# Attention with a SwiGLU gate: the first phase's maxima beside the last two projection blocks

## The chip, the cores and the metric

The kernel runs on one core of one Trainium2 chip. The metric is the device time of one execution in microseconds; of several executions the median counts. Besides them there is one profiled execution, whose time and trace are used for all reasoning about single instructions. The engines are called as in the profile: PE is the matrix engine, PEld its weight loads, DVE the vector engine, ACT the scalar engine, POOL the GpSimd engine, SP the engine that issues nearly all DMAs.

## The reference

The input is one sequence of 2048 rows of 512 numbers, normalised per row; all data are float32.

```python
def _A_ref(x, wqkv, wo):
    H = 32; Dh = D // H                       # 32 heads of 16
    qkv = (x @ wqkv).reshape(B, S, 3, H, Dh).transpose(2, 0, 3, 1, 4)
    q, k, v = qkv[0], qkv[1], qkv[2]
    scores = jnp.einsum("bhqd,bhkd->bhqk", q, k) * Dh ** -0.5
    p = _softmax(scores, axis=-1)
    o = jnp.einsum("bhqk,bhkd->bhqd", p, v)
    return o.transpose(0, 2, 1, 3).reshape(B, S, D) @ wo

def _B_ref(x, w1, w3, w2):                    # 512 -> 1792 -> 512
    return (_silu(x @ w1) * (x @ w3)) @ w2

xn = _layernorm(x)
return x + _A_ref(xn, wqkv, wo) * _silu(_B_ref(xn, w1, w3, w2))
```

Products are made of split operands: a number is kept as a high part that PE takes as it is and a low part, and a product is three matmuls (low by high, high by low, high by high; `split3`, line 184).

## The kernel before

**Opening.** Lines 345 to 481 work through four blocks of 512 rows. A block has eight projections to queries and keys (12 matmuls of 128x128 by 512 each, lines 444 to 455) and four to values (`token_values`, 12 matmuls, line 410), in the order: two projections, then one value product, four times. Behind a query or key projection ACT copies the high part out of PSUM (line 452), DVE subtracts it for the low part (line 453), and both go to DRAM over SP's queue (line 455). Blocks 0 to 2 also turn the next block's normalised rows (`transposed`, line 389). The transposed rows of a block lie in a pair of tiles, for even blocks in the opening's own pool, for odd blocks in the pool `keep`; they also go to DRAM (line 440) for the gate. `load_k` and `load_q` (lines 327 and 335) bring a head pair's keys and queries back from DRAM in six DMAs each: after block 2 the queries of pairs 0 and 1 (lines 480 and 481), in block 3 keys and queries of pair 0 and keys of pair 1 (lines 474 to 478).

**Attention.** A phase is a pair of heads and half of the queries, 32 phases in all. Head 0 of a pair works on the upper 64 rows of the array and head 1 on the lower 64 rows, so two matmuls of 64 rows run at once, in two lanes. A phase needs first its row maxima: 64 matmuls (`max_unit`, line 488), each reduced by DVE out of its PSUM bank into the tile mp (line 498). `max_rows` (line 501) joins them, turns them with PE (line 510), splits them into high and low (lines 513 and 514) and writes them with four SP DMAs as two more rows under the queries of each head (line 521). Only then the phase's 64 score matmuls can run (`scores`, line 523, they use these rows), each followed by an exponential on ACT into one of 13 tiles pt (line 533). Four exponentials make one chunk for the product with the values (`values`, line 538, accumulated in the bank pv). At the end of a phase `take_out` (line 546) copies pv to the tile ot and divides it by the sums, over several DMAs, POOL splits it (lines 567 and 568).

**Gate.** Beside attention, `gate` (line 608) is cut into half matmuls of 64 rows for the same two lanes (`Lanes`, line 702; matmul at line 757). Its weights come in 168 units of 128x512: an SP DMA (line 282), then two POOL operations that make high and low (`Weights.pump`, lines 296 and 297) in a ring of nine tiles each (`w_split`, line 206, tile pool `ring`). At most AHEAD = 5 units are split ahead.

**Closing.** The last phase (pair 15, second half) is run so that its two query halves are finished one behind the other; between them the output projection (`projecting`, line 934, 12 matmuls for each of 16 row tiles), the product with the gate and the writing of the result take place. Its inputs are fetched by `tend` in a fixed order once the last gate matmul is out (`open_tail`, line 797).

**PSUM.** Seven banks are handed out by `take` (line 156): the one that is free earliest by the kernel's own estimate, the one longest unused among equals. In the opening that is a plain rotation. The eighth bank is pv.

**Order.** What PE gets after the opening, and so the order on all engines, is written out by hand in `ORDER_OF_ISSUE` (line 44), one letter for each item: f and F a half matmul of the gate in lane 0 and lane 1, m and M one of the maxima, s and S one of the scores, v one chunk by values, R a phase's rows turned and written, r is R and v, o one tile of the output projection. A dot emits nothing: it advances the clock of `Model` (line 211), an estimate kept while the kernel is built, with which an item that is not possible yet is held back until it is (line 1124). All engines execute their instructions in the order in which they were emitted; PE waits at a matmul whose data or bank aren't ready. Memory of the opening's pool is taken over by the pools `ring`, `work` and `ffn`, whose first use waits for the last use of the old tiles, DMAs out of them included.

Of the kernel before, what the change touches and what calls it, by code (L numbers as in the profile page):

```python
# [49 lines left out]
    "MvSmMffSfFfSFffMsFsFMfsFfFmFsFFfmSfFmFmFvsMSssMvMmsSfMvsMSffMSffMfSSffMfMrSfMssFfFmFFfFmFsFsFfmFmFFm"  # L50
    "SfFfFmFsFfmSvsMMfmSvvMsfMfSFffSfFmSfFfMfSFfsFMfsFfMMfvsMMsfSvSsMsmFmFvSmFfFsFmFsFfmSfFFmmFSffFmFsFFf"
    "fMsFFffMsFfFmFmFFfSfMmvSfMfMfSfMfMfSfvSmfMMsfSvsMsMmMvvSffMSfMfSfFfSffMsFfFsFmFsFmFFfsFmFvsMSsvmSfSf"
    "FmSFffFmSfFsFFsmFfFSmfFSfFfMsFfSfMRvMsSmFmFmvSmFmMsvsFFsMmFmsFvSmMfFsmFFfFsFfMfSsFfFfMfFsFmSfFfMfsFF"
    "mFmFfMfMsvSmSmmFvmFsFFmFmSsvvsMfSSfmFfFFfSmfFMfSfSfFfMfsFsSvMsMmFmvvSfMfSfSfMffSfMfMfFfFsFsFmFmFfFsF"
    "sFmFFmFfSsvMsSmfMfMvSsMmvsMfSMfFffSFfmSfFfSmFFfSfmFFsFsMfFfmFsMfFMsvsMmMFsvvMfsFfSFmSffFMfFsFfsFMfmF"
    "SfFffSmFsFfSmFRvsMSfMsvFmmSMfvSfMfMsFsfFfFSfmFsFFfmSFfFmsFmFfFSmfFfMfMvvMffSMffSsFFfmFSfFmFfFsFmSfSf"
    "FmFfsFmFsFvSmSfsSMfvMfSsMfMfvSmMsfMvsMSffSmFfFfFmSfFmFsFmFfFsFmFfFFfMmmMvvsMsFFsFsFsFmSvMfSffMfFSfMf"
    "fSfMfFFsMfFsmFFfSfmFMvSmMmSsvSmFmFssFmFFffSFfSmFfSfFmsFFfMmFfsFMfMfvvsMsSSfrMsSfMfMmvsMMsfFFfFfsFfMF"
    "sFfFsMfSffFSmFffSmFFmFfMmvSmfSMmvsMMsFsvsMFmSfFfFsFfMfSfFmFfSfMfmFSfFfSfMfmFsFFmMvvSmSmSmvSffMMsfFsF"
    "FffSmFsFfFmFSfmFsFSffFMffFmFMsvsMMfSmvsMSsFmmFvMsFsFmFsFfFmsFfFmFSfMfSfMffFMmFfMmvvSffMfMMfSsvSmSfMf"  # L60
    "FfSffFMsFfSfMffSfFsMFffFsMfSfFFmFfsFmFSfmFrsMsMMsvsMsSvMsSmfMfMvvsMfSfMfSfMffSfSfMfSFfmFFfsFmFsFsFFf"
    "mMvvmSFfFsfMSffFmFfFSfmFsFFsMfFfSfMfFfsFmFSfsFvvSmMssMvsMSfMfFfSffFmFSffFmSSfFfmFsFFfmSfFSfFmFfFmsMv"
    "sMMfMsvsMsFsFMffFfFMsFfFsMffFSfMmvSmmFmFFsvvSmfSMfFfFsfFfMmFSffFSfsFfMFffMsFFmFfsMvSmFmFsmFvSmmSSfFf"
    "fFfFMsfFsFsFFfSfMfSfrvSmSsMsvmMsSmFvSmmFsFfSFfFfMsFfSfmFSffFmFsFmFmFvvmFSmfSSfFffFmFFsfFmFsFsFSsvvsF"
    "FsMsFfMfFfSffFSmFfFsMffSFfsMFfsFMffFmFMmvvSmsFmFFmmFSsFfFFfFsMfSffMfSFfsFmFmFmSvSmMmmSvvsMMffSfSfSfS"
    "MvMsMfsFFfsFFfsMFfFsFmSfFfMsFfSfMfFfSfMmFfFmMvvsMMfMsvsMfMSfSfFfFmfFSfmFSfSfmFFfSfMfFsFmmFFsFmFsFRvm"
    "SSmmMvSsmMvSmMfsFFffSFfMffSfFMsFsFffMsFfFSfMfmFmFFmvsMmFFsFmvMsmSmFsFvvsMSsMffFfFfMsFfFFmfSfSmFSfFfm"
    "MvvSfMffSSfSffMfMsFFfFfFsmFFssFmFFfFssFMfFfsMvMfSfSfSmvMsSmSmvsMSfmFSfFffMSfFfmFsFFsmFmFFfsFmFfFMfMf"
    "sMvSfmSmMvsMfSMmvvSmsFFsmFfFfMSfsFFfMfMfsFfSfFMfSfMfsFMfFsFmRvSmmFSmvvSmFsFfsFFmFfSfFmfFFsmSFfFfsMFf"
    "SfMffMfFmSvsMsSMmvmSfSfMfMvSmmFsFfFFfFsFfSfMfSfFfMsFfFsfMsFfFmMvsMMmFmvvmSSfSfMfFfFfmSFfFsmFsFFfsFmF"  # L70
    "fFsSFfMffSsFvMmsMMfvsMSsvMsfMsFSffFfSmFfFsMFfSffFmSfFFmFsfFFmSsFfmMvMsfMMsvvSfmSfFFfMffFSfFmmFfSFffS"
    "FfMfSffMsFFsfFmFSfFfMsRvsMSmmSvSmMsMfsvsMMmvvSfMfMffSMffSfSfMfFfFsmFFsMfFffSFmSffFMfsFfFMsFmfFsMfFmF"
    "sFfFMsvmMfSSmfFFffFSfmFmFsFvvsMsMMsvsMSffSfMfFfFfMSfMffSfSfFMfsFFfsFmFmFsFFmvSmSfMmvSmmMvSmmFsFfFfFS"
    "fFmsFmFsFfFMfsFfMFfMmvsMmMsFvsMFfmSFfSffFsMfFsFmFfSfFsMfFfFMfsFMfSmvSsMsvMmSmvSmfFfFsFFmfSmFFfSfmFsF"
    "fMfFSfMfmFfSRvMssSsMvMfSmfSfFmFFfsFmFFfmSvSmmFSmvvmFsFFmfFFsFmmFsFFfFsFmFsFfFmfSSfMffMvSmsSSmvmSFsfF"
    "mFfFsFMfFsfFmSFfsFMfSfFfMsFfMfFfvmSsMMmvvsMMffSfSfMffSfSmFfFFsFmFffSmSFfmFfFSfmFsFmFFmvsMsMsFvsMsMMs"
    "vvsMSffSMffFfFSfMfFmSfSffFmFSffFmFsFmFFmmFsFrvSmSffFMfFsFfsMfFsFmFFsFfmSFfSfSfmFfFmMvsMSfMsfMvSmSsmM"
    "vsMmMFsvvMfSmfSfFSfFfMffSfFMsfFsFMfsFFsMfFmFFssFvvMsMfSffSfMfSfmFfFSfmFsFfFmFsFfFmSmFFfSfFmfFmSvSmSm"
    "mMvvsMsFsFMfFfFfsFMsFfsFMffFSsFfMfFfMfSfMfSmFFmMvvSsMsmSvFmSmmFsFFffFSfFmFfSfFmfSFfFmSfMfmFMfFfsMvsM"
    "MfMsvvSmSfSfMffFFfMsfFSfmFsFfFMsfFmFFsfFsFSfRvSmsSMfvsMmMsFvvMsfFfMfSfFSfmSfFFfsMfFSffFmSFfsFmFsFFfm"  # L80
    "SvMsFmsFsFvvMsFfSffSMffFfSFsmFFfmSfFfSFfmFfSmFFmvMsSsMmvsMfMmMvSsMfFffFfSfMfSfMsFFfMfsFfFmMsFfFmMfFS"
    "mFFmFvSsFmMmvSmmFSmvSmFmFsfFFsFmFsFfMfSfMfFsMffFSffMfFSfMfMmvvSmMfsFFfsFFfMsFfsFMfFfSfSmFfSfFmFfSfSf"
    "mFfFMsRvsMsMMsvvMsMsfMfMvSfSfMffSMffMmvSmSfsFFfFmFfsFFmsFFfSmfFmFSffSfFMsFffFmSFfSfMfsFfFMmvMsMfMfSf"
    "vSfsMsSvmSfMfFfFsFmFMsvsMmMsFvvsFfFFsfMFssFmFfFSfMfSffFmSfFmFmFSffFSmvsMmSmFvsMfFsSMfFffFsMfFsFSfMff"
    "FsMfFSffFmMvvsSmSfFfFmFFffSfMfSfFmSfFmFfFsMfFmSvSmfMsMvsMfMfSfFfSfFmFmFsFmFsFfFsFsFmFsFrvsMfSfSfMfSv"
    "mSsMMmvsFFsFmmFFsFmFsFfSffFmFmFSfSfMffFMfSfFmFsFfSfmFvmFsMmFfSvsSsMmFvsSmFmFFsvvSmfSfMSffFFfMsFfsFmF"
    "sFFfMsFfMfFsfSfFmMFfmMvvSmfSmFFsfFFmFsFmFsFmFfSfSfFmFffSfSMfSfsFMfvmSfSMmvSmmMFsFmvsFMffFSffMFssFmFf"
    "FSffSMffFMfSfmFfFsFvMsMmFsvsMsMFmrSmMsvSmMfFsfFfSFfmSfFFmSffSfFfMFsFfmFfSfFMmvsMsSmFFmvvMsFsfFfMFsFf"
    "mFSffFMsfFSfMfFfsFMsFfMfMfvsMmSmSvsFmSmFmFvSmFffSFfFmSffFmSfFSfmFsFfFMsfFfSMffSvMssMMsvSmmMfFFsfFFfs"
    "FFmFsmFFfsFmFfFMfMfMsvSsMfMmvsMMfMfMffSvSfMsFffFFsMfMfSfSffFFsmFFfmFsFFfMfSmvSmSsvMsSmrsMMfmFFmvsMfS"  # L90
    "mFFffSFfmFsFFfFmSmFffSfMfFSfmFfSmFfFmMvvSmsSmFFfFfFmFsFsFmfFsFFmFsFmMvsMMsSffMvMfSfMffSSffMfMvSffMsS"
    "sFvMssFFsfMFffFMsfFfSfMfSFfsMFfSmFmFFfSmvSmMmmFvvSmSfmFfFFfFsmSfFSfmFFfFsFmFsFfMsFfSfMfSfvMsMsMmvvSf"
    "MfMfSffMfSsFfFMfsFsFFfMmFfMsvsMFfSfmFmFSmFfmFmFvvRSmmSFfFfFfsFFmsFFsFmFsfFFsMfFsMvmSfMfSfMfSfSMffSfM"
    "fMfSfsvsMsSMmvvsMSffSfSfSfMmvfMsFmFfFsFFmFsmFFmFsFfFsmFFfsFFmSfFmfFSfmFFsmFFfMsvSsMsmMvvSfMfSfMffMfM"
    "MfSfMffSvvSffSfMfMfSfSfMfsFFfsMFfsFMfsFFfmSFfmFFmfSfFsMvsMmMvSmFffSmFfSfFfMSfFmFmsFFfmFsFfFfMFmvSmMm"
    "sFsFvsFmMMsvsSmSfFfFmFFsfFmFFsfFSmfFFmFfSmfFMfSRvsMsMMfvSmSsvmSMsFffFfSfFMfSfMffFSffFMsfFSfMsvMfSmFm"
# [12 lines left out]
    "fmFMmvvSfmFFfSfFsSfmFfFFsFmFfFsmFmFFfmSvSmMfSfSsvMsMfmSfMvvSffMfSSffMfMsMffMsfSffFsFmFsFmFsFFfmFsFmF"
# [25 lines left out]
def raw(ap):  # L135
    return ap.bitcast(F32)
# [1075 lines left out]
```

## Time and profile before

| what | us |
|---|---|
| median of three executions | 1814.79 (1814.16 to 1815.48) |
| the profiled execution, its own time | 1813.45 |
| the span of its trace, first to last instruction | 1811.2 |
| opening ends, first matmul of the maxima | 156.07 |
| first score matmul | 205.56 |
| last matmul of the maxima | 1702.3 |

The trace counts from the first instruction, so the profiled execution's own time is 2.25 us over the span, and it lies 1.34 us under the median of the three. In the rows below a time in front is the start in the span, the next number the duration, "x" the number of instructions, and square brackets hold the idle time of the engine before the instruction and what ended it. A row of a table by stretches has the stretch, its length, and for each engine its busy time with the number of instructions, then the granted PE clock (PEclk, 1.00 is full), the share of the DMA engines and GB/s. With a line chosen, the engine columns of that table count that line alone. Matmuls overlap, so what counts on PE is the distance from start to start.

### The profile page before, as it was taken

To read this page: it belongs to the slowest core of one execution; us is meant where nothing else is said; L and a number is where in the kernel's file an instruction comes from. 1 tells how busy PE (TensorE), PEld (TensorE's weight loads), DVE (VectorE), ACT (ScalarE), POOL (GpSimd) and SP (SyncE) were. 2 spreads that over 40 slices of the span, in tenths; PEclk is the share of its full clock that TensorE was granted. 3 is DMA by queue.
4 is the path that set the end of the run, shared out by engine and by line. 5 is a ranking of instruction groups with operands and counts; after the bars stand their busy time and mean duration, and the time that the engine had idled before them with its cause. 6 is when DMAs were issued, how large, how long until landed. Compare 5 with 4: busy or idle time off the path is not lost.

```text
span 1811.2 us, 35399 instructions
## 1 busy us (share of the span) xinstructions
PE 1777.9 (98%) x13136; PEld 1034.9 (57%) x13136; DVE 1472.7 (81%) x2450; ACT 1247.7 (69%) x2360; POOL 696.7 (38%) x728
## 2 busy tenths in 40 slices
PE   7999999999999999999999999999999999999998
PEld 6886755555555555555555555555555555555445
DVE  6525988889888898888899888899888888999525
ACT  3221477777777777776787777777777778777742
POOL 2104932545055523544255505551345425542000
PEclk9999999999999999999999999999999999999999
DMA  6656212122231213132222203222313121222542
GB/s 229 239 168 168 68 39 46 53 58 68 71 91 53 60 42 72 49 66 92 55 76 56 56 25 74 52 65 90 89 45 69 48 64 42 66 74 68 176 143 87
DMA packets 130203, 147.27 MB, mean 81 GB/s; under 512 B 28016, under 2 KB 86384, under 8 KB 126960
## 3 DMA queue, kind: packets, MB, share of 16 engines
q1 hardware_dynamic: 129744, 144.51, 28.7%
q8 instruction: 103, 1.69, 0.4%
q14 instruction: 68, 0.56, 0.1%
q10 hardware_dynamic: 288, 0.52, 0.1%
HBM read 104.33 MB, written 39.58 MB: 79 GB/s over the span
## 4 chain that ended last, share of the span: by engine, by line
PE 89%; DVE 6%; issue 2%; POOL 1%; DMA 1%; ACT 1%; SPq 0%; DVEq 0%; POOLq 0%; ACTq 0%
PE pv L543 25%; PE f L757 24%; PE e L530 17%; PE m L496 13%; DVE mp L498 5%; PE e L186 2%; PE e L190 2%; PE e L188 2%; PE m L186 1%; PE m L188 1%; PE m L190 1%; PE o L186 1%; PE o L188 1%; PE o L190 1%; DVE ot L564 1%
## 5 line engine op out<-in xcount | busy, mean ns | idle before, releaser
L498 DVE TENSOR_REDUCE mp<-m 128x1 f32<-128x512 f32 x2048 | 1296.3, 684 | 172.5 <-PE m L496 89.3
L533 ACT ACTIVATE pt<-e 128x512 f32<-128x512 f32 x2048 | 1091.6, 608 | 351.4 <-PE m L496 158.2
L530 PE MATMUL e<-qs,ks 64*128 64x512 f32 x2048 | 733.5, 419 | 2.8 <-DVE mp L498 2.4
L496 PE MATMUL m<-ks,qs 62*128 62x512 f32 x2048 | 723.0, 418 | 3.7 <-DVE mp L498 2.1
L543 PE MATMUL pv<-pt,vt 128*17 128x512 f32 x4096 | 524.0, 599 | 4.4 <-ACT ot L1088 3.9
L530 PEld LDWEIGHTS e<-qs,ks 64*128 64x128 f32 x2048 | 342.2, 185 | 306.6 <-ACT pt L533 101.9
L496 PEld LDWEIGHTS m<-ks,qs 62*128 62x128 f32 x2048 | 344.1, 185 | 138.4 <-DVE mp L498 40.5
L757 PE MATMUL f<-xth,wl 64*128 64x512 f32 x896 | 313.8, 399 | 0.7 <-POOL wl L297 0.6
L757 PE MATMUL f<-xth,wh 64*128 64x512 f32 x896 | 314.4, 394 | 0.0
L757 PE MATMUL f<-xtl,wh 64*128 64x512 f32 x896 | 309.3, 395 | 0.0
L757 PE MATMUL f<-wh,hs 64*128 64x512 f32 x896 | 264.9, 397 | 1.4 <-POOL hs L645 1.1
L297 POOL TENSOR_TENSOR wl<-wr,wh 128x512 fp32r<-128x512 f32 x168 | 216.6, 1289 | 14.0
L543 PEld LDWEIGHTS pv<-pt,vt 128*17 128x17 f32 x4096 | 80.8, 96 | 196.2 <-issue 179.2
L296 POOL TENSOR_SCALAR wh<-wr 128x512 fp32r<-128x512 f32 x168 | 104.0, 619 | 158.7 <-DMA wr<-in_B_w_dram 65.3
L757 PEld LDWEIGHTS f<-xth,wh 64*128 64x128 f32 x896 | 157.3, 186 | 12.3 <-issue 1.7
L567 POOL TENSOR_SCALAR oh<-ot 128x512 fp32r<-128x512 f32 x31 | 19.5, 629 | 374.4 <-DVE ot L564 365.0
L757 PEld LDWEIGHTS f<-xth,wl 64*128 64x128 f32 x896 | 154.3, 186 | 15.5 <-issue 2.9
L757 PEld LDWEIGHTS f<-xtl,wh 64*128 64x128 f32 x896 | 154.3, 186 | 11.7 <-issue 1.7
L757 PE MATMUL f<-wl,hs 64*128 64x512 f32 x448 | 160.2, 394 | 0.0
L757 PEld LDWEIGHTS f<-wh,hs 64*128 64x128 f32 x896 | 149.7, 185 | 14.5 <-POOL hs L645 1.5
L643 POOL TENSOR_TENSOR h<-g,h 128x512 f32<-128x512 f32 x56 | 71.8, 1283 | 161.6 <-ACT h L639 157.2
L627 POOL TENSOR_SCALAR th<-th 128x512 f32<-128x512 f32 x56 | 34.6, 618 | 180.1 <-ACT th L620 180.1
(137 smaller groups left out, 1226.0 us busy)
## 6 DMA issues: line engine op xcount, KB each, us to landing
wr<-in_B_w_dram SPq DMA_DIRECT2D x168, 256.0 KB
qs<-qk SPq DMA_DIRECT2D x192, 64.0 KB
ks<-qk SPq DMA_DIRECT2D x96, 128.0 KB
qk<-sh SPq DMA_DIRECT2D x32, 256.0 KB
qk<-sl SPq DMA_DIRECT2D x32, 256.0 KB
xin<-in_A_x_dram SPq DMA_DIRECT2D x16, 256.0 KB
g<-part SPq DMA_DIRECT2D x16, 256.0 KB
rb<-rd SPq DMA_DIRECT2D x124, 32.0 KB
```

The lines of the kernel that those rows point to most:

```text
L186: nc.tensor.matmul(ps, lhs[1], rhs[0], start=first, stop=False)
L188: nc.tensor.matmul(ps, lhs[0], rhs[1], start=False, stop=False)
L190: nc.tensor.matmul(ps, lhs[0], rhs[0], start=False, stop=last)
L296: nc.gpsimd.tensor_scalar(hi, t, 1.0, 1.0, op0=ALU.mult, op1=ALU.mult)
L297: nc.gpsimd.tensor_sub(lo, t, raw(hi))
L496: nc.tensor.matmul(ps, qs[p % 2][64 * h:64 * h + KM, q0:q0 + P], ks[p % 2][64 * h:64 * h + KM, c * 512:(c + 1) * 512], start=True, stop=True)
L498: nc.vector.reduce_max(mp[p, half][:, h, qt, c:c + 1], ps, axis=AX.X)
L530: nc.tensor.matmul(ps, ks[p % 2][64 * h:64 * h + KR, k * P:(k + 1) * P], qs[p % 2][64 * h:64 * h + KR, q0:q0 + 512], start=True, stop=True)
L533: nc.scalar.activation(pt, ps, AF.Exp, scale=DH ** -0.5)
L543: nc.tensor.matmul(pv[32 * j:32 * j + VW, :], vt[:, key, 2 * p + j % 2, :], pt, start=key < 2 if last else k == 0, stop=key >= NT - 2 if l ...
L643: nc.gpsimd.tensor_mul(h2, g, h2)
L757: nc.tensor.matmul(ps, left[r], right[r], start=starts and lane == 0, stop=ends and lane == 1)
```

## The change

The first phase's maxima move from the order table into the opening. `early` lists them by 512 keys at a time, and `beside` puts them in groups of 6, 4 or 2 behind projections and value products of blocks 2 and 3 (the second number in `groups` is the place in the block, 0 to 11). Behind the last group the three steps of `max_rows` follow at places 9, 10 and 11, counted as calls with a place of 8 or more. The keys and queries needed are loaded earlier and keys in parts: queries and the first 1024 keys of pair 0 after block 1, the next 512 keys after block 2, the last 512 in block 3; the keys of pair 1 are loaded one projection group earlier than before. The even blocks' transposed rows move to a pair of tiles "xe" in `keep`, which afterwards serves as the first four places of the weight ring, so that four weight units can be split by POOL during block 3 (`wts.pump(KC)`). The other five places of the ring are tiles of their own. The model's clock starts anew after the opening. `max_unit` and `max_rows` are otherwise unchanged; their small tiles lie in `keep`.

The order table is another one: 4032 half matmuls of the gate, 2048 scores, 512 chunks by values and 22 output tiles as before, but 1984 maxima in place of 2048, and 29 dots in place of 15. Before, 210 gate halves and 80 maxima stand ahead of the first score; after, 3 and 2.

```diff
 ORDER_OF_ISSUE = (
-    "mMmMmMmM.fMffMffMffMffMffMfM.fMffMfm.MmFFfFffFFffFFffFfFmFmFFfmMmFfFfFFmfFFmFmmMffFfMffFmFFffMfmFm.M"
...
-    "SsSSvvsSSsSsvSsvoSssSSsovsSsSsSvSsoovvooooSsSssSovsSsSovvsSoooooosSSsSosSosSsvsSsSvsSSvvv..........."
+    "MfMffSSfMffMsMsMffMfSfvSffMfSfSMffMfMfFfFfFsFmFsFsFfFmFfFsMfFsFfMmvsMSmmSvSfMfMfMsvsMfMFffFMsfFfFmSF"
...
+    "mFmsFsFsFFmFsFFmFFsFsSmFFmFFmSsFvSmSmMsvMssSSvmSsSSvMsSsvmSSsvmSSsFsvsMsSSvMsSsSvMsSsFsFsFFvM......."
+    "........oSsoRvSsSssoSvSsSsSsSvsSSovSssSSsvvsSsSsSvSsovsSsSSssvsoSssSvSsosvvoS........oooooSsSsSsvoSs"
+    "SvSvooooooSssSosSSsosSvsSsSvSsSvvv......"
 )
...
+    slots, turns = {}, {"h": 0, "l": 0}
+
     def w_split(v):
-        return ring.tile([P, 512], F32R, tag=f"w{v}", name=f"w{v}", bufs=RING)
+        if not slots:
+            slots.update(zip("hl", even_pair()))
+        i = turns[v] % RING
+        turns[v] += 1
+        if i < KC:
+            return slots[v][:, i, :]
+        return ring.tile([P, 512], F32R, tag=f"w{v}{i}", name=f"w{v}{i}", bufs=1)
+
+    def even_pair():
+        return [keep.tile([P, KC, 512], F32R, tag=f"xe{v}", name=f"xe{v}", bufs=1) for v in "hl"]
...
-        def pump(self):
+        def pump(self, ahead=AHEAD):
-            while self.split < min(len(self.units), self.taken + AHEAD):
+            while self.split < min(len(self.units), self.taken + ahead):
...
-    def load_k(p):
+    def load_k(p, cols=slice(0, S)):
...
-                xts[b] = xt_pair(keep if b % 2 else pro)
+                xts[b] = xt_pair(keep) if b % 2 else even_pair()
...
+        early = iter([(0, 0, 4 * qt + c, h) for c in range(4) for qt in range(8) for h in range(2)])
+        groups = {(2, n): 6 for n in range(1, 11, 2)}
+        groups.update({(2, 11): 2, (3, 2): 6, (3, 3): 6, (3, 4): 4, (3, 6): 6, (3, 7): 6, (3, 8): 4})
+        first_rows = max_rows(0, 0)
+
+        def beside(b, n):
+
+            for _ in range(groups.get((b, n), 0)):
+                max_unit(*next(early))
+            if b == TB - 1 and n >= 8:
+                next(first_rows, None)
...
                     for s, st in enumerate((sh, sl)):
                         nc.sync.dma_start(raw(qk_d[rbk][s])[:, b * 512:(b + 1) * 512], raw(st))
+                    beside(b, 3 * i + v)
...
                 if b > 0:
                     token_values(b, i)
+                    beside(b, 3 * i + 2)
...
                     if i == 0:
-                        load_k(0)
+                        load_k(0, slice(3 * 512, S))
                         wts.start()
+                        load_k(1)
                     if i == 1:
                         load_q(0, 1)
-                        load_k(1)
-            if b == TB - 2:
+                        wts.pump(KC)
+                        wts.fill()
+            if b == 1:
                 load_q(0, 0)
+                load_k(0, slice(0, 2 * 512))
+            if b == 2:
+                load_k(0, slice(2 * 512, 3 * 512))
                 load_q(1, 0)
...
     lanes = Lanes()
     free_at[:] = [0.0] * BANKS
+    mod.start()
+    wts.there = dict.fromkeys(wts.there, 0.0)
     wts.pump()
...
-    ready = {}
+    ready = {0: 0.5}
-    count = {"S": 0, "M": 0, "V": 0, "chunks": 0, "phase": 0}
+    count = {"S": 0, "M": 64, "V": 0, "chunks": 0, "phase": 1}
```

More of the change, by code (lines that the diff above doesn't have):

```diff
@@ L50 @@
[L50 to L84, printed above, removed]
@@ new lines @@
+    "MmvMssFMffFfFsMsfSfmFmFFffSfSmfFfSFsvmSmFmSvsFmFsFFmFsFfmFsFMfFfSfMfSfMfvmSSsSmvmFsSmMvsMMffMfSfFfFS"
+    "fMffFMfsFMfmFFfsFfFSmvSmsFsFmFvmFsMsMvSmSfMfFfsFfMSfFfmSfFFsmFsFfFmSFfMfSfFfmMsvsMMmFmvvSmfFFfmSFffS"
+    "mFsFfFMsFfsFFmsFFfMfMfFfSfsMvrSfMffSSfMffMsFfFfMMsvsMMfsFFffSFmsFfFmFFmFsFfFfMffMfSfSvMsSmSfvmSsFsFm"
+    "FfFfFmFfSfFMsFfsFmFmFFfSmvSmmSSsvvMsMmvsMfMfMFffSfFSffFSfmFsFfFmSFfFmsFFfmFsMFfsMvvMsSfmFmFFfFfmFsFS"
+    "ffFFmFsfFMfsFfMfMMfFfSfMfSfvSmsMMsvSmMmSfSffMmvvSmMfMfMffSSffSffMFfFfsFFmFsmFFsFffMsFfFmSmFfFmSvSsmM"
@@ L216, in __init__, with start @@
         def __init__(self):
+            self.start()
+        def start(self):
             self.lane, self.begun = [0.0, 0.0], [0.0, 0.0]
@@ L330, in load_k @@
             r = (p % 4) * 32 + h * DH
-            kh, kl = (raw(v)[r:r + DH, :] for v in qk_d[4 + p // 4])
+            kh, kl = (raw(v)[r:r + DH, cols] for v in qk_d[4 + p // 4])
             for n, src in enumerate((kh, kl, kh)):
-                nc.sync.dma_start(raw(t)[64 * h + n * DH:64 * h + (n + 1) * DH, :], src)
+                nc.sync.dma_start(raw(t)[64 * h + n * DH:64 * h + (n + 1) * DH, cols], src)
     def load_q(p, half):
```

192 lines of the change are left out of this document (110 added, 82 removed).

## The prediction

> **What bounds the kernel now.** I read the page first, then a table over the five stages, then the same table for single lines, then the timeline at the two ends of the first maxima.
>
> ```profile
> PE 1777.9 (98%) x13136; PEld 1034.9 (57%) x13136; DVE 1472.7 (81%) x2450; ACT 1247.7 (69%) x2360; POOL 696.7 (38%) x728
> PE 89%; DVE 6%; issue 2%; POOL 1%; DMA 1%; ACT 1%; SPq 0%; DVEq 0%; POOLq 0%; ACTq 0%
> ```
> ```profile
> 87.00:122.00 35.00, 35.00 (x161) 28.42 (x160) 10.70 (x20) 8.99 (x16) 1.09 (x2) 1.00 0.47 181
> 122.00:156.00 34.00, 34.00 (x147) 27.13 (x145) 5.53 (x8) 7.04 (x12) 0.00 (x0) 1.00 0.95 227
> 156.00:205.50 49.50, 45.79 (x292) 31.51 (x291) 46.78 (x81) 7.23 (x13) 43.64 (x46) 0.93 0.28 81
> 205.50:1702.30 1496.80, 1491.62 (x11731) 830.06 (x11729) 1317.46 (x2183) 1156.67 (x2191) 623.11 (x643) 1.00 0.25 64
> 1702.30:1811.20 108.90, 95.64 (x477) 56.66 (x476) 40.62 (x68) 40.45 (x81) 6.87 (x7) 0.94 0.39 128
> ```
>
> PE is busy almost throughout and makes 89% of the chain that ended last. The 6% of DVE sit in one place: from 156.0 to 205.5 DVE is busy 46.78 of 49.5 us while ACT has nearly nothing to do. These are the first phase's maxima, before which no score can run. Busy time says little of PE there, so I count its items. With the gate's line alone (first two rows), then the maxima (two), the scores and the values:
>
> ```profile
> 156.00:205.50 49.50, 40.53 (x210) 28.00 (x210) 0.93 0.28 81
> 205.50:1702.30 1496.80, 814.26 (x3824) 565.80 (x3822) 1.00 0.25 64
> 156.00:205.50 49.50, 31.26 (x80) 14.83 (x80) 0.93 0.28 81
> 205.50:1702.30 1496.80, 691.19 (x1967) 329.11 (x1967) 1.00 0.25 64
> 205.50:1702.30 1496.80, 716.23 (x1974) 334.35 (x1974) 1.00 0.25 64
> 205.50:1702.30 1496.80, 499.69 (x3936) 76.65 (x3936) 1.00 0.25 64
> ```
> ```profile
> 168.07 0.40 PE L757 MATMUL f<-xtl,wh 64*128 64x512 f32 x2
> 168.31 0.39 PE L757 MATMUL f<-xth,wh 64*128 64x512 f32 x2
> 217.39 1.84 PE pv L543 x16
> 238.26 0.98 PE pv L543 x8
> ```
>
> A pair of half matmuls, one in each lane, starts every 0.23 us (168.07, 168.31). The first stage holds 210 + 80 halves, 145 pairs, 33.4 us of work in 49.5 us: 16 us of PE are lost there. The long stage holds 3824 + 1967 + 1974 = 7765 halves, 3882 pairs, 893 us, and 3936 / 8 = 492 chunks by values, which then cost (1496.8 - 893) / 492 = 1.23 us each, their turns included. A chunk alone spans 0.98 us and two in a row 1.84 us, so 0.86 us is the price of a further one. This stage is bound by PE and runs evenly; what is added to it costs its pairs.
>
> **Part 1, the stage that goes.** The opening ends at 156.07. All that follows the first score stays, and the 210 gate halves and 16 of the 80 maxima, 113 pairs, move behind the start of the scores: 113 x 0.23 = 26.0 us at the plain rate. The new table is a little denser. Between groups of v the longer lane holds 3915 letters in sum in the old table (from the first score to the last maximum) and 4024 in the new one (from its beginning): 109 slots more, 25.1 us. It has 387 groups of v in place of 397. A group costs (1496.8 - 3915 x 0.23 - 492 x 0.86) / 397 = 0.44 us beyond its letters, so ten fewer save 4.4 us. The stage becomes 1496.8 + 25.1 - 4.4 = 1517.5 us; 1522.8 at the plain rate is the bound on the other side. I take 1517.5, because the same count gives the old stage.
>
> **Part 2, the groups in the opening.** Blocks 2 and 3 are 35.0 and 34.0 us of PE without a gap, so every moved matmul lengthens them. The 64 maxima are 32 pairs, 7.4 us.
>
> ```profile
> 152.94 0.40 PE L190 MATMUL e<-xth,wqh 128*128 128x512 f32 x1
> 153.38 0.59 ACT L452 CAST sh<-e 128x512 fp32r<-128x512 f32 x1 [2.21 <-PE e L190]
> 154.00 0.69 DVE L453 TENSOR_TENSOR sl<-e,sh 128x512 fp32r<-128x512 f32 x1 [2.11 <-ACT sh L452]
> 155.75 0.40 PE L190 MATMUL m<-wqh,xth 128*128 128x512 f32 x1
> 156.07 1.24 PE L496 MATMUL m<-ks,qs 62*128 62x512 f32 x7
> 158.61 13.85 DVE L498 TENSOR_REDUCE mp<-m 128x1 f32<-128x512 f32 x23 [3.93 <-DMA wr<-in_B_w_dram]
> 1720.23 0.50 PE L530 MATMUL e<-qs,ks 64*128 64x512 f32 x2
> 1720.65 0.50 PE L186 MATMUL o<-ks,xtl 128*128 128x512 f32 x1
> ```
>
> Going from whole-array matmuls to halves takes 0.32 us from start to start (155.75 to 156.07), 0.09 over a slot; back takes 0.42 us (1720.23 to 1720.65), 0.19 over. Twelve groups make 3.4 us of turns, so 10.8 us is the lower bound. Then the banks: seven rotate, and a group of six behind a projection gives the next product the projection's own bank. Its last matmul starts at 152.94 and DVE is done with it at 154.69; with the signal that is 1.82 us later, while the group itself ends 0.32 + 0.46 + 0.42 = 1.20 us later. Such a group therefore costs 1.82 - 0.23 = 1.59 us. Seven are of this kind (block 2 at places 1, 3, 7, 9, block 3 at 3, 6, 7): 11.1 us. Behind value products only ACT's copy is waited for, which ends earlier. Place 5 of block 2 costs 0.97, and 0.6 for DVE, which is late there with normalising; 11 of block 2 costs 0.5, places 2, 4 and 8 of block 3 0.97, 0.74 and 0.74: together 4.5 us. DVE reduces one maximum in 13.85 / 23 = 0.60 us, six in 3.6, which is longer than one product (12 x 0.23 = 2.8): two groups in a row at places 6 and 7 add 0.2, the turned rows at place 9 0.3.
>
> ```profile
> 121.53 5.47 SPq L342 DMA_DIRECT2D qs<-qk  x12
> ```
>
> Twelve loads take SP 5.47 us to issue. The same number now stands ahead of block 2, where the first group is due two products and a transposition (about 6 us) after its start: about 0.7 us late. Other moved DMAs have most of a block's time, and what SP issues later behind them (the writes of xt, sh and sl, x) is not waited for within that block. The four split units cost nothing, as POOL is idle in block 3; without that cover the gate's first unit would be some 2 us late. Sum: 11.1 + 4.5 + 0.5 + 0.7 = 16.8 us. The upper bound is no cover for DVE at all, 64 x 0.60 = 38.4 us; DVE is busy 16.2 us of the 69 in these blocks, 54.6 of 86 with them, so I stay near the lower end.
>
> **Part 3, the new start.** The first score now stands three slots into the order, and needs the four row DMAs.
>
> ```profile
> 154.71 0.32 SPq L455 DMA_DIRECT2D qk<-sl  x1
> 201.03 0.80 SPq L521 DMA_DIRECT2D qs<-mh  x1
> 203.26 0.64 SPq L521 DMA_DIRECT2D qs<-ml  x1
> 205.56 0.49 PE L530 MATMUL e<-qs,ks 64*128 64x512 f32 x1
> 159.36 0.79 PE L496 MATMUL m<-ks,qs 62*128 62x512 f32 x1 [2.05 <-DVE mp L498]
> 159.00:166.00 7.00, 6.03 (x23) 4.75 (x24) 7.00 (x13) 0.00 (x0) 6.67 (x8) 0.51 0.29 82
> PE e L186 <- DVE wql L406: 2.3, 1, 2.3
> 36.00:43.00 7.00, 4.71 (x23) 3.51 (x22) 4.83 (x8) 1.86 (x4) 2.30 (x2) 1.00 0.60 196
> ```
>
> They are issued on SP behind the last projection's writes, whose last issue ends at 155.03, 1.0 us before the opening does. The four take 2.9 us (201.03 to 203.90), and the score came 4.5 us after the first. So it can start 1.8 us (landing at once) to 3.5 us after the opening; PE reaches it after 0.7 us and waits 1.1 to 2.8 us, with all items behind it. I take 2.6, because the sl write just ahead needs long itself: DVE's first reduce waited until 158.61, 3.9 us after 154.71.
>
> The clock: a gap of 2.05 us ending at 159.36 was followed by a stretch at 0.51; a wait of 2.3 us in the opening, between 36 and 43, left it at 1.00. Seven us at half speed cost 3.4 us. With both outcomes seen at this length I take 0.7 of it, 2.4 us; bounds 0 and 3.4. [...]
>
> **Part 4, the closing.** Its items are the same (74 scores, 20 chunks, the output tiles), so 108.9 us.
>
> ```profile
> 1721.97 0.66 ACT L549 COPY ot<-pv 128x512 f32<-128x512 f32 x1
> 1751.91 1.26 POOL L568 TENSOR_TENSOR ol<-ot,oh 128x512 fp32r<-128x512 f32 x1
> 1753.84 2.39 PE L543 MATMUL pv<-pt,vt 128*17 128x512 f32 x8 [3.88 <-ACT ot L1088]
> 1753.00:1760.00 7.00, 6.16 (x22) 1.69 (x23) 0.00 (x0) 5.60 (x11) 0.17 (x1) 0.51 0.63 210
> ```
>
> PE waits 3.88 us for the tile ot, taken from 1721.97 until POOL's last read ends at 1753.17, and loses 3.4 us of clock. The new order has five whole output tiles and the sums in that place instead of four, about 3 us more cover, so some of 7.3 us may go. Against it, the gate now ends two letters ahead of the last maximum instead of 63, so the closing's fetches start some 20 us later relative to it, and the table plans 23 dots within (15 and 8), 5.3 us at 0.23, perhaps with 3.4 us of clock. Bounds -7.3 and +8.7; I take +1, near the middle.
>
> **Sum.** 156.1 + 16.8 + 2.6 + 2.4 + 1517.5 + 108.9 + 1 = 1805.3 us of span against 1811.2: 5.9 us less. From the median of 1814.79 that leaves 1809 us.
>
> **Rivals.** *The start doesn't stall and the closing gains:* clock as in the row of 2.3 us (-2.4), ot in time (-7.3 in place of +1). Together 1798 us. For it speaks the longer cover; against it the dots. *The closing gives it back:* fetches late, +8.7 in place of +1, 1817 us; with half of it 1813, no measurable change. For it: twenty microseconds of head start are gone, and SP is in order. Against: 12 chunks and 8 tiles, 12 x 1.23 + 8 x 2.8 = 37 us, stand between the last maximum and the second run of dots. *Slower by DVE:* if the subtraction behind each of the seven projections finds the six reduces of the group before still running, PE waits 3.6 + 0.7 - 2.8 = 1.5 us more at each, 10.5 us in all: 1819 us. It decides from 0.9 us at each on. For it: a group of six is 3.6 us of DVE, a product 2.8, and DVE takes them in order. Against: DVE has 31 us to spare there, and most groups have a product without a group between them. *The loads come late*, so that maxima wait for keys at several groups: the DMA share in block 3 is 0.95, and 3 us at each of three loads make 1818 us; that change would then not do what it says.
>
> **Chances.** The forecast with its own range 1803 to 1813: 0.50, of which 0.12 lies within 0.2%. Start and closing gain: 0.16. The closing gives it back: 0.17, of which 0.08 within 0.2%. DVE 0.12, loads 0.05, both slower. About 0.2% (3.6 us) is what a measurement of this kernel can tell from no change. Faster: 0.38 + 0.16 = 0.54; same 0.20; slower 0.09 + 0.17 = 0.26. The range of 1800 to 1819 leaves out about 0.1 on each side.
>
> **What would show it.** Blocks 2 and 3 together should last about 86 us, with PE waits of about 0.6 us behind seven groups, on DVE's line 453. The first score should come some 3 us after the opening, ahead of it a gap of over 2 us, and the clock shows whether that halved it. From there to the last maximum 1517 us and from it to the end 110. The forecast is wrong if the two blocks exceed 92 us, if the long stage exceeds 1523, or if the closing exceeds 115.

## The result, and the profile after

The changed kernel takes 1822.39 us (median of six executions, 1820.19 to 1824.18) where the kernel before, run beside it, takes 1814.47 us (six, 1812.27 to 1815.60). The ratio is 1.0044, with an interval of 1.0031 to 1.0057: 0.4% slower, where 0.3% faster was forecast, and above the range. The profiled execution took 1820.19 us, its span is 1818.0 us.

First the page's line of engines and its chain. Then the table of busy time by stretches of the changed kernel: the two blocks with the moved maxima, the start, the long stage and the closing.

```profile
PE 1772.4 (97%) x13136; PEld 1036.2 (57%) x13136; DVE 1476.8 (81%) x2450; ACT 1250.9 (69%) x2360; POOL 698.0 (38%) x728
...
PE 90%; DVE 3%; DMA 2%; issue 1%; SPq 1%; POOL 1%; ACT 1%; DVEq 0%; POOLq 0%; ACTq 0%
```
```profile
87.50:131.00 43.50, 41.23 (x188) 30.52 (x187) 28.63 (x50) 9.20 (x16) 1.10 (x2) 1.00 0.44 160
131.00:174.00 43.00, 41.60 (x185) 29.78 (x183) 26.97 (x46) 7.05 (x12) 7.56 (x8) 1.00 0.57 176
174.00:177.20 3.20, 1.03 (x8) 0.57 (x7) 1.29 (x2) 0.59 (x1) 0.00 (x0) 0.90 0.10 28
177.20:1701.50 1524.30, 1514.82 (x11950) 857.28 (x11950) 1328.21 (x2192) 1164.83 (x2202) 659.55 (x678) 1.00 0.25 62
1701.50:1818.00 116.50, 97.60 (x479) 56.81 (x477) 40.12 (x67) 41.84 (x83) 7.87 (x9) 0.90 0.45 152
```

DVE's 6% of the chain have become 3%, so the stage that waited for the first maxima is gone. PE works 5.5 us less than before, but stands idle for 1818.0 - 1772.4 = 45.6 us where it was 1811.2 - 1777.9 = 33.3. The stages beside the prediction's, from the same instructions:

| stage | before | forecast | after |
|---|---|---|---|
| opening, to the first matmul behind it | 156.1 | 172.9 | 174.0 |
| from there to the first score | 49.5 | 2.6, and 2.4 of clock | 3.1, and 1.4 of clock |
| first score to last maximum | 1496.8 | 1517.5 (+2.4) | 1524.3 |
| last maximum to the end | 108.9 | 109.9 | 116.5 |

The 2.6 us are the wait alone, and 2.2 us of it came; the clock's share shows up in the row below. The opening and the start are as forecast, within 1.1 us each. Of the 12.7 us of span between forecast and result, 11.0 lie in the last two rows with the clock counted in. PE's waits, longest in total first, name the places:

```profile
PE m L447 <- DVE xn L438: 9.1, 2, 7.1
PE e L565 <- DMA qs<-ml: 7.6, 2, 5.5
PE m L369 <- DVE mp L371: 6.3, 6, 3.9
PE e L565 <- ACT pt L568: 4.9, 1, 4.9
...
PE m L447 <- DVE sl L518: 1.0, 2, 0.5
PE e L186 <- DVE sl L518: 1.0, 2, 0.5
PE m L186 <- DVE sl L518: 0.9, 2, 0.5
```

The columns after the colon are the sum in us, the number of waits and the longest one. The first row lies at the start of the opening and was there before, with 8.9 us. The three last rows are six waits of about 0.5 us behind groups in the opening, as Part 2 gave them. The three rows between hold four long waits: for the first phase's rows (2.2 at 175 us), for DVE in the middle of the long stage (3.9), and two in the closing (5.5 and 4.9). The wait of 2.2 us was forecast, and the one of 4.9 us was there before, with 3.88. The other two are new.

**The wait of 3.9 us at 888 us.** The timeline of the changed kernel around it, SP's queue first, then rows of ACT, DVE and PE:

```profile
876.93 0.45 SPq L732 DMA_DIRECT2D xth<-xt  x1
877.43 0.42 SPq L732 DMA_DIRECT2D xtl<-xt  x1
877.95 2.71 SPq L348 DMA_DIRECT2D ks<-qk  x6
882.14 5.40 SPq L590 DMA_DIRECT2D sums<-ot  x4
```
```profile
875.35 0.59 ACT L584 COPY ot<-pv 128x512 f32<-128x512 f32 x1 [1.39 <-POOL hs L679]
891.21 0.25 DVE L592 RECIPROCAL rec<-sums 128x16 f32<-128x16 f32 x1 [5.63 <-DMA sums<-ot]
891.38 1.22 DVE L371 TENSOR_REDUCE mp<-m 128x1 f32<-128x512 f32 x2
887.62 0.50 PE L369 MATMUL m<-ks,qs 62*128 62x512 f32 x1
892.07 0.79 PE L369 MATMUL m<-ks,qs 62*128 62x512 f32 x1 [3.94 <-DVE mp L371]
```

At the end of a phase `take_out` copies pv (875.35) and sends the sums through SP to another layout. Here those four small DMAs stand behind two loads of 1 MB for the gate's next rows and six of keys. SP waits 4.3 us in total for the two large loads while it issues them, from 882.14 to 887.54, and they land only for 891.21. DVE's reciprocal waits 5.63 us for them, and behind it, in DVE's order of issue, wait the reduces that would empty PE's banks (the next runs at 891.38). PE runs dry at 888.12. The clock goes to half speed within the gap (0.50 from 889.94) and stays there behind it, as the table by stretches shows (the second row is the closing):

```profile
889.90:896.90 7.00, 4.83 (x18) 1.93 (x20) 4.47 (x8) 2.35 (x5) 0.00 (x0) 0.51 0.27 78
1719.30:1726.30 7.00, 5.77 (x20) 2.56 (x21) 0.00 (x0) 4.51 (x9) 0.00 (x0) 0.51 0.69 231
```

PE works only from 892.07 on, so about 4.8 us of the 7 cost clock: 3.94 + 4.8 x 0.49 = 6.3 us together.

**The wait of 5.5 us in the closing.** The last phase's rows, from the maximum to the score:

```profile
1702.96 0.17 DVE L379 TENSOR_SCALAR nm<-mx 128x16 f32<-128x16 f32 x1
1708.15 0.27 PE L383 MATMUL m<-ident,nm 128*16 128x128 f32 x1
1710.05 0.28 DVE L387 TENSOR_TENSOR ml<-m,mh 16x128 fp32r<-16x128 f32 x1
1720.53 0.79 PE L565 MATMUL e<-qs,ks 64*128 64x512 f32 x2 [5.45 <-DMA qs<-ml]
```
```profile
1709.62 0.43 SPq L892 DMA_DIRECT2D x<-in_A_x_dram  x1
1715.53 0.73 SPq L394 DMA_DIRECT2D qs<-mh  x1
```

The maxima are ready at 1703.13. PE turns them only at 1708.15, since the table has two output tiles ahead of the R. The halves are ready at 1710.33, but SP still has eight loads of 256 KB (from 1709.62; rows of x and of the gate's result, for the output tiles) ahead of the four row DMAs. In the old order the gate ended 63 letters ahead of the last maximum and not two. The same eight loads were issued there from 1693.49 on, 8.8 us ahead of the last maximum; here it is 8.2 us behind it.

### The profile page after: what moved, and what is told of

It reads as the page before. It is cut to its first block, busy times and chain, and to the rows that moved or that the text cites. A ratio compares the mean times of both kernels' runs of the same rounds, so it can differ in the third digit from the quotient of the medians.

```text
span 1818.0 us, 35385 instructions
## 1 busy us (share of the span) xinstructions
PE 1772.4 (97%) x13136; PEld 1036.2 (57%) x13136; DVE 1476.8 (81%) x2450; ACT 1250.9 (69%) x2360; POOL 698.0 (38%) x728
## 4 chain that ended last, share of the span: by engine, by line
PE 90%; DVE 3%; DMA 2%; issue 1%; SPq 1%; POOL 1%; ACT 1%; DVEq 0%; POOLq 0%; ACTq 0%
PE pv L578 26%; PE f L792 25%; PE e L565 17%; PE m L369 13%; DVE mp L371 2%; PE e L186 2%; PE e L190 1%; PE e L188 1%; PE m L186 1%; PE m L188 1%; PE m L190 1%; PE o L186 1%; DMA ks<-qk 1%; PE o L188 1%; PE o L190 1%
## 5 line engine op out<-in xcount | busy, mean ns | idle before, releaser
L792 PE MATMUL f<-xth,wl 64*128 64x512 f32 x488 | 176.9, 399 | 0.0
L792 PE MATMUL f<-xtl,wh 64*128 64x512 f32 x488 | 173.6, 393 | 0.0
L792 PE MATMUL f<-xth,wh 64*128 64x512 f32 x488 | 172.3, 393 | 0.0
L792 PE MATMUL f<-wh,hs 64*128 64x512 f32 x496 | 155.7, 396 | 0.0
L792 PE MATMUL f<-xth,xel 64*128 64x512 f32 x408 | 148.9, 398 | 0.0
L792 PE MATMUL f<-xth,xeh 64*128 64x512 f32 x408 | 146.2, 394 | 0.0
L792 PE MATMUL f<-xtl,xeh 64*128 64x512 f32 x408 | 144.5, 392 | 0.0
L792 PE MATMUL f<-xeh,hs 64*128 64x512 f32 x400 | 124.5, 395 | 0.4 <-POOL hs L680 0.4
L312 POOL TENSOR_TENSOR wl<-wr,wh 128x512 fp32r<-128x512 f32 x92 | 118.5, 1288 | 7.7
L312 POOL TENSOR_TENSOR xel<-wr,xeh 128x512 fp32r<-128x512 f32 x76 | 98.3, 1294 | 6.3
```

What stands on the lines that cost most here:

```text
L312: nc.gpsimd.tensor_sub(lo, t, raw(hi))
L792: nc.tensor.matmul(ps, left[r], right[r], start=starts and lane == 0, stop=ends and lane == 1)
```

## The experiments

Each run is compared with runs of the kernel before on the same chip. The edits are to the changed kernel, unless said otherwise.

| run | median us | ratio to before, interval | span of the profile |
|---|---|---|---|
| the change | 1822.39 | 1.0044 (1.0031 to 1.0057) | 1818.0 |
| e1, old order | 1825.11 | 1.0060 (1.0048 to 1.0073) | 1822.9 |
| e2, later reciprocal | 1813.06 | 0.9999 (0.9991 to 1.0008) | 1810.6 |
| e3, last rows first | 1813.56 | 0.9998 (0.9989 to 1.0007) | 1810.9 |
| e4, first rows earlier | 1824.81 | 1.0051 (1.0039 to 1.0064) | 1823.3 |
| e5, three mends and an exponential | 1807.12 | 0.9965 (0.9953 to 0.9977) | 1804.8 |
| e6, e5 and sooner rows of reciprocals | 1800.05 | 0.9919 (0.9905 to 0.9932) | 1797.5 |
| e7, that edit in the kernel before | 1808.88 | 0.9970 (0.9958 to 0.9981) | 1805.8 |
| e8, e6 and groups of four | 1795.67 | 0.9897 (0.9883 to 0.9910) | 1793.4 |
| e9, e8 and a queue for the last writes | 1794.58 | 0.9892 (0.9876 to 0.9909) | 1791.8 |

**e1: the new opening under the old order.** The letters of the old table stand in place of the new ones; from them the first 32 m, 32 M, the first R and four dots are taken out, nothing else. (No step by values is among them.)

> The changed kernel with the old table of letters, from which only the first phase's maxima, its rows and four values steps are taken out. Theory (the new opening is worth its price, the loss sits in where the new order puts things later): opening 174 us as in the changed kernel, a stage from the first score to the last maxima of about 1497 us as before the change, a closing of about 109 us, no gap at 888 us, so a span near 1806 us and a time near 1808, 0.3 to 0.4 per cent under the kernel before. Rival (the new opening itself, its tiles and its splitting of weights, slows what follows): the stage stays near 1524 us or the time stays at 1820 or more.

It took 1825.11 us, so the theory as put here is wrong, and the time is one that the rival allowed. Its table by stretches, and the first 100 us behind the opening in three kernels (e1, before, after), PE's items in brackets behind the first column of busy time:

```profile
174.70:200.20 25.50, 23.95 (x137) 19.58 (x137) 7.36 (x12) 3.91 (x7) 18.45 (x20) 1.00 0.37 105
200.20:1713.90 1513.70, 1507.77 (x11823) 843.51 (x11819) 1317.64 (x2182) 1160.20 (x2197) 642.09 (x661) 1.00 0.25 64
...
174.60:274.60 100.00, 97.73 (x688) 68.69 (x689) 59.33 (x98) 49.89 (x93) 70.97 (x73) 1.00 0.24 67
```
```profile
156.00:256.00 100.00, 96.29 (x697) 64.06 (x698) 92.73 (x156) 44.96 (x84) 78.33 (x81) 0.97 0.25 71
```
```profile
174.00:274.00 100.00, 97.83 (x754) 56.14 (x753) 86.77 (x145) 73.87 (x139) 50.78 (x53) 0.98 0.20 56
```

There is no gap at 888 us and the closing is 109 us, as expected of the old order. But from the end of the opening to the last maximum it takes 25.5 + 1513.7 = 1539.2 us, against 1546.2 before: 7.0 us less for 64 half matmuls moved away, which are 32 pairs or 7.4 us of work, for an opening 18.6 us longer. The start of the old order is still thin, 688 items of PE in 100 us, near the 697 of before; the new table has 754 there, in spite of its wait at the start. In part e1 makes this itself: the maxima taken out leave the other lane empty, and in the first 9.4 us 36 gate halves start one by one with six maxima beside them. So e1 shows that the opening does not pay under the old letters, not what it would return under an old order with full lanes. That the opening slows what follows, the rival, is not borne out by e2, which has the same opening. The gain of the change appears only with the new table, which runs scores and values beside the gate from the first slot on. My expectation took the old stage's 1496.8 us over unchanged, although half of what preceded it was gone.

**e2: the reciprocal a step later**, in the one half of a pair where the wait stands.

```diff
         yield
+        if (p, half) == (6, 1):
+            yield
         nc.vector.reciprocal(rec, sums)
```

> The changed kernel; only in the second half of the seventh pair of heads VectorE's reciprocal of the sums is issued one step of the normalisation later. Theory (VectorE stands 5.6 us in its order at that reciprocal, which waits for sums that queue behind loads on SP, and TensorE runs dry at 888 us): the gap of 3.9 us there and the 6.8 us of half clock behind it go, about 7.3 us less, a time near 1815. Rival (TensorE there is held by something else, such as the banks): the gap stays above 2 us and the time within 2 us of the changed kernel's 1822.

The span falls by 7.4 us to 1810.6, the median by 9.3 (the change's profiled execution was itself the shortest of its six, and e2's eleven executions spread from 1812.37 to 1817.97). In the long stage itself it is 7.0 us, 0.7 more than the gap and its clock add up to; where those 0.7 us come from is open. The timeline of DVE and the long stage in the table by stretches:

```profile
893.56 0.24 DVE L594 RECIPROCAL rec<-sums 128x16 f32<-128x16 f32 x1
```
```profile
178.20:1695.50 1517.30, 1511.68 (x11949) 856.89 (x11949) 1328.42 (x2192) 1164.80 (x2201) 659.97 (x678) 1.00 0.25 63
```

The reciprocal runs 2.35 us later than in the changed kernel and nothing waits for it; PE has no gap there, and no half clock. The stage is 1517.3 us, near Part 1's 1517.5, once the collision is out of it. That they meet within 0.2 us is partly luck, since 1.7 us of half clock from the start lie in the 1517.3 and not in the count.

**e3: the last phase's rows first.** The place is the one behind the last maximum; the letters are those of the table.

```diff
-...............oSsoRv
+...............SsRoov
```

> The changed kernel; in the last phase the turn and the rows of the maxima are issued ahead of two output tiles and of the loads for the next token block. Theory (the rows' DMAs stand on SP behind loads and an output tile): the gap of 5.45 us at 1715 us and the half clock behind it go, up to 8.8 us less, a closing of 108 to 110 us in place of 116.5 and a time near 1814. Rival (the loads that now come later are missed by the output tiles instead): a gap of the same size at the next output tile, a closing of 114 us or more.

```profile
1708.74 0.71 SPq L394 DMA_DIRECT2D qs<-mh  x1
```
```profile
PE m L383 <- ACT pt L568: 1.1, 1, 1.1
```

The rows are issued 6.8 us earlier, the wait of 5.45 us is gone from the list of waits of the closing, a new one of 1.1 us for the turn's bank stands there, and the closing takes 108.4 us. The loads that were overtaken are not missed. The edit moves the turn and the row DMAs at once. In the changed kernel the halves were ready 5.2 us before the first row DMA was issued, nearly the whole wait of 5.45 us, so the trace puts it down to the loads on SP; no run moves the DMAs alone.

**e4: the first phase's rows ahead of the last projection's writes.**

```diff
+                    if (b, 3 * i + v) == (TB - 1, 10):
+                        next(first_rows, None)
                     for s, st in enumerate((sh, sl)):
```

> The changed kernel; the DMAs of the first phase's rows are issued ahead of the writes of the last projection's two halves in place of behind them. Theory (the first score waits for rows whose DMAs stand behind those writes): the gap of 2.17 us at 175 us shrinks under 0.7 us and the half clock behind it goes, about 3.5 us less, a time near 1819. Rival (the first score waits for its keys or its exponent's bias from elsewhere): the gap keeps over 1.5 us, the time moves by less than 1 us.

The first score runs 0.6 us behind the opening instead of 3.1, and then PE stops 1.3 us later. So the wait for the rows goes as expected, but the gain does not come. (The three steps of `max_rows` run at the places 8, 9 and 10 of block 3, so the row DMAs stand right behind the last projection's writes.) The timeline of ACT and PE's waits between 173 and 186:

```profile
175.19 0.59 ACT L468 COPY vt<-m 128x512 f32<-128x512 f32 x1 [2.21 <-PE m L190]
178.90 1.57 ACT L570 ACTIVATE pt<-e 128x512 f32<-128x512 f32 x3 [3.12 <-DMA wr<-in_B_w_dram]
```
```profile
PE m L369 <- ACT pt L570: 2.6, 1, 2.6
```

ACT begins its first exponential 3.1 us after its last copy, so the banks fill. The start has a second wait close behind the first. In the closing its wait for the rows is 6.4 us in place of 5.5, and the clock is at half speed in two stretches of 10.2 us, so its time is no measure of the edit.

**e5: e2, e3 and e4 together, and an exponential of a 128x1 tile early in block 3**, to try whether ACT's pause belongs to the first exponential.

```diff
+        one = pro.tile([P, 1], F32, tag="one", name="one")
+        nc.gpsimd.memset(one, 0.0)
...
                     beside(b, 3 * i + v)
+                    if (b, i, v) == (TB - 1, 0, 0):
+                        nc.scalar.activation(one, one, AF.Exp)
```

> The changed kernel with the later reciprocal, the last phase's rows ahead of the output tiles, the first phase's row DMAs ahead of the last projection's writes, and one exponential of a 128x1 tile early in the last projection block. Theory: the terms add, 9.3 us of the reciprocal and 8.8 us of the last rows, as the two runs showed them, and at the start both waits are gone: with the row DMAs earlier the first score ran 3.1 us sooner but ScalarE then issued its first exponential 2.81 us after its last copy had ended; if that pause belongs to the first exponential after copies, the early one takes it into the opening and no gap over 0.7 us is left near 175 us, about 3 us less. Sum: 1822.4 - 9.3 - 8.8 - 3 = 1801, range 1798 to 1805. Rival (the pause is a wait for something else that comes at its own time): the gap of 2 to 2.6 us stays and the time is 1803 to 1806. Second rival (the mends shift each other's order in time and a collision comes back): 1808 or more, with a new gap over 3 us.

1807.12 us, outside the range I gave and 1.1 us above the first rival's. The spans nearly add: e2 and e3 took 7.4 and 7.1 off 1818.0, e5 13.2. Of the 21.1 us expected of the median 15.3 came. The 3 us at the start did not: the gap there is 2.79 us, ACT's first exponential again 3.3 us after its last copy. The rest, 2.8 us, is less than what the medians of e2 and e3 had fallen beyond their spans (9.3 + 8.8 against 14.5); why they did is open. The first rival's mechanism is the likelier one: an early exponential does not take the pause away, and e9 shows what it waits for.

**e6 and e7: the read-back of the reciprocals a step sooner**, for the wait of 4.9 us that the kernel before has too, with 3.9. The copy of the last values into the tile ot (line 1125) waits until the half before has left that tile.

```diff
         nc.vector.reciprocal(rec, sums)
-        yield
+        if (p, half) != (NP - 1, 0):
+            yield
         nc.sync.dma_start(rd.rearrange("j (a b) -> (j a) b", b=16), rec)
```

> The four mends and, for the last but one half alone, the reciprocals' write to memory issued in the same step as the reciprocal, so that the rows of reciprocals are read back 4 us sooner, ahead of the loads for a later token block. Theory (the gap of 4.9 us that stands in the closing, 3.9 us before the change, is ScalarE's copy of the last values waiting for the tile that these rows hold): the gap shrinks under 1 us and the half clock behind it goes, 7 to 8 us less than with the four mends alone. Rival (the copy waits for something else, or the loads ahead hold the rows as long): within 2 us of the four mends alone.

> The kernel before with that last edit alone. Theory: the same gap stands there (3.88 us at 1750 us, then 6.8 us of half clock), so it gains up to 7 us, a time near 1808; then that gain is no part of the change. Rival: no gain, within 1 us of 1814.5.

The timelines of SP and DVE, e5 first, then e6:

```profile
1729.39 0.35 SPq L900 DMA_DIRECT2D inh<-in_A_x_dram  x1
1733.13 2.66 SPq L605 DMA_DIRECT2D rb<-rd  x4
1741.56 0.69 DVE L969 SCALAR_TENSOR_TENSOR res<-xel,o 128x512 f32<-128x512 f32 x1 [1.36 <-PE o L190]
1742.89 0.69 DVE L607 TENSOR_TENSOR ot<-ot,rb 128x512 f32<-128x512 f32 x1
```
```profile
1727.91 1.76 SPq L606 DMA_DIRECT2D rb<-rd  x4
1733.81 0.69 DVE L608 TENSOR_TENSOR ot<-ot,rb 128x512 f32<-128x512 f32 x1 [1.94 <-DMA rb<-rd]
1734.21 0.37 SPq L901 DMA_DIRECT2D inh<-in_A_x_dram  x1
```

Behind eight loads of 256 KB the four rows are issued 5.2 us later and took 9.8 us to their use, ahead of the loads 5.9. Not all of that is the queue: in e5 the DMA engines fall idle at about 1738.5, and the product then stands in DVE's order behind two operations on an output tile, of which the first waits for PE until 1741.56. In e6 the rows land in time for the product to run ahead of those operations. The wait falls from 4.9 to 1.5 us, and the closing from 109.0 to 102.3. The time falls by 7.1 us; in the kernel before the same edit brings 1814.2 to 1808.88. That gain is no part of the change.

**e8: e6 with groups of four.**

```diff
-        groups = {(2, n): 6 for n in range(1, 11, 2)}
-        groups.update({(2, 11): 2, (3, 2): 6, (3, 3): 6, (3, 4): 4, (3, 6): 6, (3, 7): 6, (3, 8): 4})
+        groups = {(2, n): 4 for n in (1, 2, 4, 5, 7, 8, 10, 11)}
+        groups.update({(3, 2): 6, (3, 3): 4, (3, 4): 4, (3, 5): 4, (3, 6): 4, (3, 7): 4, (3, 8): 6})
```

> The kernel with the four mends and the sooner rows, and the first phase's maxima in groups of four in place of six (eight groups in block 2; in block 3 five of four and two of six). Theory (a group of six waits about 0.5 us for banks of its own, a group of four does not): groups of four cost 0.75 us as the changed kernel's two of them did, 13 x 0.75 + 2 x 1.57 = 12.9 us in place of 15.8, so the first main matmul comes 2 to 3 us sooner and the time falls by as much. Rival (each stop of the projections costs a fixed amount, so more groups cost more): the opening is 0 to 2 us longer.

PE's waits between 87 and 182, all of them, and the table at the start:

```profile
PE m L369 <- ACT pt L574: 1.7, 1, 1.7
PE m L369 <- DMA ks<-qk: 1.1, 1, 1.1
PE m L383 <- DVE nm L379: 0.8, 1, 0.8
```
```profile
176.20:179.50 3.30, 3.30 (x17) 1.37 (x17) 1.89 (x3) 1.86 (x4) 3.13 (x4) 0.50 0.60 170
```

None of the six waits for the projection's bank is left. The opening ends 1.4 us sooner than in e6, less than the 2 to 3 expected: three more turns of the array, and 0.8 us at the turn of the rows, as DVE now has six reduces from the last group in place of four. The other 3 us of the time are in the closing (102.3 to 100.6), where the 1.5 us wait went, and in the start, whose gap is 1.7 us in place of 2.6.

**e9: the last projection's two writes on ACT's queue.**

```diff
-                        nc.sync.dma_start(raw(qk_d[rbk][s])[:, b * 512:(b + 1) * 512], raw(st))
+                        (nc.scalar if (b, i, v) == (TB - 1, 3, 1) else nc.sync).dma_start(raw(qk_d[rbk][s])[:, b * 512:(b + 1) * 512], raw(st))
```

> The kernel with the mends, the sooner rows and the groups of four; the writes of the very last projection's two halves go out on ScalarE's own DMA queue in place of SP's, where they stand behind the first phase's rows. Theory (ScalarE's first exponential waits until the opening's last writes have landed, since its tile lies in the memory of the opening's tiles: it started 3.9 us after the last of them was issued, in three runs): the first exponential starts within 1 us of ScalarE's last copy, the gap of 1.68 us near 175 us goes with its half clock, 2 to 3.4 us less, a time near 1793. Rival (the first exponential waits for something else): the gap stays over 1.2 us and the time within 1 us of 1795.7.

The 3.9 us there run to ACT's first recorded wait; to the start of the exponential itself it was 4.2 to 4.4 us. ACT's timeline and the long stage:

```profile
172.18 0.33 ACTq L524 DMA_DIRECT2D qk<-sl  x1
173.63 0.59 ACT L468 COPY vt<-m 128x512 f32<-128x512 f32 x1 [2.21 <-DMA qk<-sh]
174.95 1.57 ACT L574 ACTIVATE pt<-e 128x512 f32<-128x512 f32 x3 [0.73 <-DMA qk<-sl]
```
```profile
173.50:1690.90 1517.40, 1511.62 (x11957) 853.56 (x11956) 1328.86 (x2194) 1165.17 (x2203) 658.72 (x678) 1.00 0.25 63
```

The exponential comes 0.73 us after the copy and its releaser is now one of these writes; the gap and its half clock are gone, and from the end of the opening to the last maximum it takes 1517.4 us, 2.9 less than in e8. The span falls by 1.6 us only, as the opening of this execution is 1.1 us longer (it has a stretch of half clock at 42 us, where the traces of the kernel before and of the change show 1.00); the median falls by 1.1. So the exponential waits for the writes. Why they land sooner is open: seen from the end of the opening they are issued no earlier than in e8, but SP's weight loads of 256 KB, which followed them 0.5 us later there, start 1.9 us behind them here. This version has the lowest median, within the spread of e8, 1.1% under the kernel before; e7 shows that some 5 us of that would be had without the change.

## Why the prediction was wrong

**What bounds the kernel: right.** The 16 us of PE lost before the first score were there, and the change removes them. With the collision away (e2) the stretch from the opening to the last maximum falls from 1546.2 to 1520.5 us. Of these 25.7 us, 7.0 are there in e1 too, under the old letters with their lanes partly empty; the other 18.7 come only with the new table.

Two steps failed: Part 1 gave a collision in the new order no price, and Part 4 put the closing at +1 where it was +7.6. Both signs that the forecast named for them came, a long stage over 1523 us and a closing over 115. Either one alone would have left the time inside the range.

**Part 1, the stage: the count was right, its use was not.** Letters and groups counted to 1517.5 us and e2 measured 1517.3. The step that failed is to price the new order by its density alone. The count takes for granted that every wait lies as well covered as in the old stage, and a new table shifts every small step in time against SP's loads. One of 32 normalisations met two loads of 1 MB and six of keys, and cost 7.0 us. No rival had this, although the rows on DVE's order and SP's queue that it needs were at hand.

**Part 2, the groups: right.** Sixteen point eight us forecast, 17.9 measured from opening to opening, with six waits of 0.5 us where seven of 0.6 were given. The rival of a late DVE there (10.5 us) did not come, nor that of late loads: one wait of 0.7 us.

**Part 3, the start: right by its numbers, incomplete in its cause.** The gap is 2.17 us (2.6), the clock cost 1.4 (2.4). The 2.17 us gap was followed by half speed (0.50 from 176.55 to 179.96), as the one of 2.05 us was in the kernel before (0.50 from 159.05 to 165.88). Behind the rows, a second wait lay hidden: the first exponential's tile lies in memory of the opening's tiles, and waits for the opening's last writes. Only e4 uncovered it, and e9 removed both.

**Part 4, the closing: the term was mis-sized.** I took +1 between -7.3 and +8.7; it was +7.6. The rival that the closing gives it back had the right mechanism, fetches that come late on SP, and its 8.7 us; e3 shows 8.1. Its argument against was wrong: 37 us of PE's work between the last maximum and the second run of dots do not help, because the transfers hit the last phase's rows at once, behind the first run, where two output tiles stand ahead of the turn. The gain of 7.3 us, more cover for ot, did not come: the wait grew to 4.9 us.

**The sum.** 1.1 us of the opening, 5.0 between the opening and the last maximum (7.0 of collision against 2.0 saved elsewhere) and 6.6 of the closing make the 12.7 us of span. Each of the two late ones alone, taken out, leaves a kernel equal to before (e2, e3); both out make it 0.35% faster (e5, whose two further edits did not remove the start's gap). That is the trade that the forecast described, at 7 us instead of 6.

## What to carry to other kernels

When an order written out by hand is replaced, its length in slots says what it costs if nothing collides. Go through the small in-order steps that were tuned to the old one (a reciprocal that waits for 2 KB behind megabytes in the same queue, the rows at the last phase), and give the chance that one of them now waits a price of its own: a gap and the half clock that can come with it (here 3.94 us and 2.4). A wait that is removed at a start can have a second one right behind it (in e4 one of 2.6 us); list all that the first instruction of each engine waits for, freed memory among it.

## What the runs showed of the hardware

In these runs the half clock does not follow from the length of the gap alone. A gap of 1.68 us was followed by 0.50 (e8, from 176.2), one of 1.49 us in e6's closing was not (1.00 from 1742.8 to 1750.0), and e4's of 2.56 us was not:

```profile
179.60:186.40 6.80, 6.80 (x53) 4.99 (x55) 5.28 (x9) 4.95 (x10) 5.66 (x6) 1.00 0.54 156
```

A gap of 2.29 us near 40 us is in all eleven traces. In six of them (e2, e3, e4, e5, e7, e9) half speed followed; in the other five none did (in the kernel before and in the change the clock is 1.00 from 36 to 43). What decides between the two outcomes was not shown.

The gap of 4.91 us in the closing, the same in five kernels, was followed by a stretch of 6.8 us at half speed in the changed kernel (from 1756.92), e2, e3 and e5, and by one of 10.2 us in e4. The part of a stretch that lies within the gap costs nothing more (in the changed kernel 3.05 us, to 1759.97, in which PE is idle). A gap of 2 to 5 us therefore cost itself here and anything from 0 (e4's 2.56 us) to at most 5 us (e4's closing, 10.2 x 0.49).
